# A transformer block on one core: FFN steps on 128 rows, a tabled order of the kernel's head, and other tables for PV

## The chip, the cores and the metric

The kernel runs on one core of a Trainium2 chip. The metric is the device time of one execution in microseconds (us), the median over several runs. TensorE (PE) does matrix products and loads its stationary operand in separate instructions (PEld); VectorE (DVE) and ScalarE (ACT) do elementwise work; GpSimd (POOL) does small operations and issues some DMAs; SyncE (SP) issues most DMAs and DMA transpositions.

## The reference

The block has 2048 rows of 1024 elements in bf16, an attention with 32 heads of 32 elements that share one K and one V, and a gated FFN with 3584 hidden elements.

```python
q = (ln(x) @ wq).reshape(B, S, 32, 32)           # 32 heads
k, v = ln(x) @ wk, ln(x) @ wv                    # one K and one V for all heads
p = softmax(einsum("bhqd,bkd->bhqk", q, k) * 32 ** -0.5)
h = x + einsum("bhqk,bkd->bhqd", p, v) @ wo
g, u = ln(h) @ w_gate, ln(h) @ w_up              # 1024 -> 3584 each
out = h + (sigmoid(g) * u) @ w_down
```

`ln` takes away a row's mean and divides by the root of its variance.

## The kernel before, in words

**Units.** Rows come in 16 tiles of 128 and 8 chunks of 256 (two tiles). Attention is cut into 64 groups; a group is one tile of 128 rows with 8 heads, in the order of the table ORDER, tile by tile after the first two. A group has 8 bursts, one for each 256 keys, so there are 512 bursts. `s_burst` (L658) is 8 score matmuls on 32 array rows each, four side by side; ACT then does two exps of 128x1024 (`one_exp`, L681). When a group's exps are there, `pv_group` multiplies them with V (L783, 32 array columns each, four side by side) and with ones for the softmax sum: either directly (L780) or, in groups that are `summed`, after DVE has added pairs of tiles (L722) and merged these sums (L731), in one or two sum items (L762). DVE then empties the bank (L801, L802), takes the reciprocal and multiplies into QT (L807 to L813).

**The other work.** K, V and Q projections (L323 on `zone`, where the transposed rows and wq lie), the output projection `wo_group` (L323 on `wo`), whose result is added to x (L873) and normalised (`stats2`, L904 to L913, POOL's powers at L349 and L351, L355), a DMA transposition of these rows on SP's queue (`transpose2`, L492), and the FFN of a chunk. A FFN step is one block of 256 hidden elements: gate (L971, then tanh on ACT, L990), up (L971, then the product on DVE, L1010). After 14 blocks come four down groups of 28 matmuls (L1035, added on DVE at L1045, stored from SP). Sigmoid is written through tanh.

**Memory.** PSUM has six banks for scores (S_ps) and two (X_ps) for everything else, so of PV, projections and FFN two groups are open at a time. The blocks of w_gate and w_up (512 KB each, "halves" in the code) are loaded on SP's queue into any free buffer of `halves`: four in wgu from the first chunk on, one more in QT after each chunk, nine in Pr and one in kT4 at the end. They are loaded anew for each chunk. w_down takes the place of the transposed rows and of wq in `zone`: 14 loads on POOL's queue (`load_wd`), each when its place is free.

**Order.** The program is written out by a planner at build time, which keeps a clock for each engine. The *head*, written out by hand, has the first 25 bursts: three groups side by side (HG = 3) and the first burst of the fourth. Each of its iterations p has three bursts, the V projection of 256 keys, two PV items of group 0, the K projection of the next keys and the normalisation of two more tiles (`ln1_step`). `zeros` are matmuls on a tile of zeros (L426). After the head a loop decides at each step what PE does next: a burst as soon as ACT is due for one; PV items; an open output group that is `first`; a new PV group; else the next group from `next_group`, which takes the output projection if its rows are ready, then what is left of q_list, then the FFN. The FFN's next step is taken when both tiles of its chunk are transposed and its block is expected within 0.3 us.

PV_PLAN has one letter for each attention group. c and e start a group right behind the first burst for which it is ready; d and e hold a burst back when the running PV group would be done within PV_HOLD; an upper case letter gives one sum item and one merge more instead of two sum items. `urgent(c)` tells that Q is done and the FFN has come to chunk c, with at most NEAR down groups to go; then output groups and their normalisation go first. WD_GAP is the number of bursts between w_down loads after Q is done. `dma` keeps a model of SP's transfers at 220 KB per us.

## Time and profile before

| | us |
|---|---|
| median of 3 runs | 1105.14 (1104.99 to 1105.42) |
| the profiled execution | 1105.36 |
| its span | 1103.5 |
| first exp starts / last exp ends | 13.8 / 1009.5 |
| last Q projection / first FFN matmul | 164.1 / 164.3 |
| first FFN matmul of chunks 1 to 7 | 294.4, 419.2, 543.5, 667.9, 791.9, 912.7, 1027.5 |
| transposition of the second tile of chunks 0 to 7 issued | 152.0, 280.3, 406.3, 530.0, 655.0, 779.4, 903.2, 1021.5 |
| last six w_down loads issued | 164.8, 175.6, 187.6, 200.1, 211.7, 223.6 |
| changes between score, PV and full matmuls on PE | 1101 |

The span is what the profile's parts cover; the execution's own time has 1.9 us around it. A busy share of PE holds the pipelined ends of matmuls, so how long one takes of PE is read from the distance of two starts, not from its duration. The granted clock is 1.00 in all stretches of the profile.

### The profile page before, as it was taken

Reading aid. Unit: us, or ns where it says so; the run is one execution under the profiler, and the core shown is the slowest. Engines: PE = TensorE matmul, PEld = TensorE weight load, DVE = VectorE, ACT = ScalarE, POOL = GpSimd, SP = SyncE. Lnnn points to the kernel's source line nnn. Section 1 sums busy time; section 2 is a strip of 40 time slices with the busy share of each in tenths; the row PEclk is TensorE's granted clock in tenths of the full one; section 3 lists DMA queues with packets and bytes.
Section 4 is the critical chain, followed back from the end, with each engine's and each line's share of the span. In section 5 each row is a group of like instructions: output and inputs, shape, how many; then the busy total and the mean of one; then the engine's idle time right before and its main releaser. Section 6 shows DMA issues by size and latency. Waiting matters only on the chain.

```text
span 1103.5 us, 32984 instructions
## 1 busy us (share of the span) xinstructions
PE 1077.9 (98%) x14253; PEld 659.5 (60%) x14315; DVE 876.1 (79%) x1574; ACT 1005.7 (91%) x1150; POOL 68.8 (6%) x142
## 2 busy tenths in 40 slices
PE   7899999999999999999999999999999999999998
PEld 6663446674476636674576546674576546674784
DVE  7769978888879888888888888888879888886111
ACT  6999999999999999999999999999999999995110
POOL 4510100100000000000000000000000000000000
PEclk9999999999999999999999999999999999999999
DMA  8951207681367515592276515582277515672920
GB/s 219 159 168 57 78 20 207 197 238 50 81 195 176 160 30 152 155 223 62 66 204 180 160 30 150 156 222 65 69 206 179 158 30 150 179 202 70 263 63 20
DMA packets 282065, 150.38 MB, mean 136 GB/s; under 512 B 38592, under 2 KB 276160, under 8 KB 281920
## 3 DMA queue, kind: packets, MB, share of 16 engines
q1 hardware_dynamic: 276256, 138.17, 47.3%
q0 software_dynamic: 2544, 9.44, 2.6%
q8 instruction: 113, 1.85, 0.7%
q10 hardware_dynamic: 3120, 0.66, 0.3%
q14 instruction: 32, 0.26, 0.1%
HBM read 136.18 MB, written 4.19 MB: 127 GB/s over the span
## 4 chain that ended last, share of the span: by engine, by line
PE 77%; ACT 10%; DVE 8%; issue 3%; POOL 1%; DMA 1%; DVEq 0%; ACTq 0%
PE X_ps L971 36%; PE X_ps L1035 13%; PE S_ps L658 12%; PE X_ps L783 8%; ACT Pr L681 8%; PE X_ps L323 7%; DVE pairs L731 3%; DVE pairs L722 2%; PE X_ps L762 1%; ACT hact L681 1%; DVE st L370 1%; ACT QT L681 0%; DMA zone<-hn 0%; PE X_ps L780 0%; DVE hx L873 0%
## 5 line engine op out<-in xcount | busy, mean ns | idle before, releaser
L681 ACT ACTIVATE Pr<-S_ps 128x1024 bf16<-128x1024 f32 x992 | 936.3, 1140 | 2.1 <-issue 1.3
L722 DVE TENSOR_TENSOR pairs<-Pr 128x1024 bf16<-128x1024 bf16 x479 | 324.3, 683 | 59.4 <-ACT Pr L681 56.4
L731 DVE TENSOR_TENSOR pairs<-pairs 128x1024 bf16<-128x1024 bf16 x397 | 273.6, 689 | 23.6 <-DVE pairs L722 0.5
L971 PE MATMUL X_ps<-QT,wgu 128*128 128x256 bf16 x2096 | 265.9, 273 | 0.1
L971 PEld LDWEIGHTS X_ps<-QT,wgu 128*128 128x128 bf16 x2096 | 193.1, 98 | 55.0 <-issue 31.3
L1035 PE MATMUL X_ps<-zone,hact 128*128 128x512 bf16 x850 | 207.0, 380 | 6.9 <-issue 5.6
L658 PE MATMUL S_ps<-QT,kT 32*128 32x256 bf16 x4096 | 203.4, 273 | 7.7 <-ACT kT L515 3.0
L971 PE MATMUL X_ps<-QT 128*128 128x256 bf16 x1328 | 167.4, 273 | 0.0
L658 PEld LDWEIGHTS S_ps<-QT,kT 32*128 32x128 bf16 x4096 | 60.9, 92 | 154.0 <-ACT Pr L681 133.4
L971 PEld LDWEIGHTS X_ps<-QT 128*128 128x128 bf16 x1328 | 123.7, 98 | 29.9 <-issue 15.6
L1035 PEld LDWEIGHTS X_ps<-zone,hact 128*128 128x128 bf16 x896 | 77.6, 97 | 102.4 <-issue 25.5
L783 PE MATMUL X_ps<-Pr,V 128*32 128x256 bf16 x3968 | 131.1, 273 | 0.9 <-DVE hact L1010 0.7
L990 ACT ACTIVATE gu<-X_ps 128x512 f32<-128x512 f32 x112 | 78.1, 698 | 57.6 <-PE X_ps L971 57.6
L1010 DVE SCALAR_TENSOR_TENSOR hact<-gu,X_ps 128x512 bf16<-128x512 f32 x112 | 76.3, 682 | 45.6 <-PE X_ps L971 44.7
L783 PEld LDWEIGHTS X_ps<-Pr,V 128*32 128x32 bf16 x3968 | 98.2, 96 | 21.7 <-issue 9.3
L323 PE MATMUL X_ps<-zone 128*128 128x512 bf16 (+3 forms) x576 | 77.9, 276 | 3.9 <-DMA zone<-hn 2.3
L323 PE MATMUL X_ps<-wo,QT 128*128 128x512 bf16 x240 | 61.4, 380 | 1.3 <-issue 0.8
L338 POOL CAST mean<-mv 128x1 f32<-128x1 bf16 x28 | 10.3, 366 | 825.1 <-DVE mv L908 815.1
L323 PEld LDWEIGHTS X_ps<-zone 128*128 128x128 bf16 x576 | 38.1, 97 | 33.9 <-issue 14.1
L801 DVE COPY ols<-X_ps 128x256 f32<-128x256 f32 x64 | 27.0, 421 | 26.3 <-PE X_ps L762 23.7
L1045 DVE SCALAR_TENSOR_TENSOR hx<-X_ps,hx 128x512 bf16<-128x512 f32 x32 | 21.9, 684 | 27.1 <-PE X_ps L1035 27.0
L323 PEld LDWEIGHTS X_ps<-wo,QT 128*128 128x128 bf16 x256 | 22.3, 97 | 28.6 <-issue 8.2
(76 smaller groups left out, 454.5 us busy)
## 6 DMA issues: line engine op xcount, KB each, us to landing
wgu<-in_B_w_gate_dram SPq DMA_DIRECT2D x73, 512.0 KB, 5.0
wgu<-in_B_w_up_dram SPq DMA_DIRECT2D x58, 512.0 KB, 4.9
QT<-in_B_w_up_dram SPq DMA_DIRECT2D x49, 512.0 KB, 5.0
QT<-in_B_w_gate_dram SPq DMA_DIRECT2D x34, 512.0 KB, 4.8
zone<-in_B_w_down_dram POOLq DMA_DIRECT2D x14, 512.0 KB, 5.4
hx<-in_A_x_dram SPq DMA_DIRECT2D x16, 256.0 KB, 4.3
out_dram<-hx SPq DMA_DIRECT2D x32, 128.0 KB, 1.7
Pr<-in_B_w_gate_dram SPq DMA_DIRECT2D x5, 512.0 KB, 7.1
```

What stands on the lines that cost most here:

```text
L323: ins = pe.matmul(sel(bank), lhsT=a, rhs=b, start=(i == 0), stop=(i == last))
L658: ins = pe.matmul(S_ps[:, bank, kt * QC:(kt + 1) * QC], lhsT=kT4[DH * j:DH * (j + 1), (2 * b + kt) * P:(2 * b + kt + 1) * P], rhs=QT[DH * ...
L681: c_e.inc(act.activation(out=p_tile(k, n % 2), in_=S_ps[:, 2 * pr:2 * pr + 2, :].rearrange("p a (b q) -> p (a b) q", q=QC), func=ACTF.Exp, ...
L722: add_half[k] = slot_use[slot] = c_dve.inc(dve.tensor_tensor(out=pairs[:, slot, :].rearrange("p (j q) -> p j q", j=4), in0=p4[:, :, 0, :], ...
L731: slot_use[x] = slot_use[y] = c_dve.inc(dve.tensor_tensor(out=pairs[:, x, :], in0=pairs[:, x, :], in1=pairs[:, y, :], op=ALU.add), T_ADD, ...
L783: ins = pe.matmul(bank[DH * j:DH * (j + 1), 0:QC], lhsT=V[:, 2 * b + kt, :], rhs=rhs(j), start=first and is_sum, stop=last and plain, tile ...
L801: dve.tensor_copy(out=ols[:, 0:QC], in_=bank[:, 0:QC])
L971: ins = pe.matmul(bank[:, j * QC:(j + 1) * QC], lhsT=halves[i][:, dt, j * P:(j + 1) * P], rhs=QT[:, dt, c * QC:(c + 1) * QC], start=(dt == ...
L990: tanh_val[n] = c_act.inc(act.activation(out=slot, in_=bank, func=ACTF.Tanh, scale=0.5), T_TANH, 0.1)
L1010: hact_val[(c, 2 * fp + 1)] = gu_read[n] = c_dve.inc(dve.scalar_tensor_tensor(out=hact[:, 2 * fp:2 * fp + 2, :], in0=slot.rearrange("p (a ...
L1035: ins = pe.matmul(bank, lhsT=hact[:, ft, tt * P:(tt + 1) * P], rhs=wd[:, ft, dc * 512:(dc + 1) * 512], start=(ft == 0), stop=(ft == NFT - 1))
L1045: v = c_dve.inc(dve.scalar_tensor_tensor(out=hv, in0=bank, scalar=0.5, in1=hv, op0=ALU.mult, op1=ALU.add), 0.61, 0.08)
```

## The change

**FFN steps.** The FFN's list now has pairs of blocks. When both tiles of a chunk are ready, a pair becomes gate, gate, up, up on 256 rows. When only the first tile is, it becomes one gate and one up group on 128 rows with both blocks in a bank, and a second such step for the other tile is put ahead of the chunk's down groups; its four blocks are loaded again, after the chunk's other loads. While that waits for the second tile, down groups of the first may run.

```diff
+                if x[0] == "pair":
+                    _, c, m = x
+                    ts, fs = UNITS[c], [2 * m, 2 * m + 1]
+                    if rows_ready(ts, now):
+                        if not halves_ready([(c, 0, 0, fs[0])], now):
+                            return None
                         ffn_list.popleft()
+                        n = [new_step(c, ts, [f], 0) for f in fs]
+                        ffn_list.extendleft([("u", n[1]), ("u", n[0]), ("g", n[1]), ("g", n[0])])
+                    elif rows_ready(ts[:1], now) and halves_ready([(c, 0, 0, f) for f in fs], now):
+                        ffn_list.popleft()
+                        n = new_step(c, ts[:1], fs, 0)
+                        ffn_list.extendleft([("u", n), ("g", n)])
+                        ffn_list.insert([i for i, y in enumerate(ffn_list) if y[0] == "down"][0], ("later", c, m))
+                        i = len([u for u in half_list if u[0] <= c])
+                        for u in reversed([(c, 1, w, f) for w in range(2) for f in fs]):
+                            half_list.insert(i, u)
...
-                            ins = pe.matmul(bank[:, j * QC:(j + 1) * QC], lhsT=halves[i][:, dt, j * P:(j + 1) * P],
-                                            rhs=QT[:, dt, c * QC:(c + 1) * QC], start=(dt == 0), stop=(dt == DT - 1))
+                            ins = pe.matmul(bank[:, j * m:(j + 1) * m], lhsT=halves[i][:, dt, j % 2 * P:(j % 2 + 1) * P],
+                                            rhs=QT[:, dt, r0:r0 + m], start=(dt == 0), stop=(dt == DT - 1))
```

`rows_ready` and `halves_ready` ask the planner's clock for the transposed rows and the blocks. Output groups are now listed by tile, and tile 1's are no longer always `first`.

**Head.** A table says what stands in each of its 21 places: V a V projection, u or U the next of HEAD_U and then of the eight 256-row groups of chunk 1's Q (u emptied by ACT, U by DVE), W the first 512-row Q group, P a PV item, L an `ln1_step`, z four zero matmuls.

```diff
+    HEAD = ['uuL', 'V', '', '', 'LVLu', 'UU', 'PP', 'LWL', 'zu', 'PPL', 'VV', 'uLPLz', 'PPVL', 'U', 'UPL', 'Pz', 'U', 'UP', 'PzP', 'VV', 'PPU']
+    HEAD_U = [5, 6, 4, 7]
...
             for p in range(1, BPG):
                 k0 = HG * p + 1
                 s_burst(k0)
                 exps(k0)
-                g1 = vq_group(p, [])
-                run_group(g1)
-                run_item(pv[0])
-                run_item(pv[0])
-                zeros(3, pv[0])
-                ln1_step(2 * p + 4)
+                head(3 * p - 2, p)
                 s_burst(k0 + 1)
                 exps(k0 + 1)
-                q = p + 2
-                if q > HG:
-                    g1 = vq_group(None, [q]) if q < NQ else q_group(q - NQ, QC, QC)
-                    run_group(g1)
-                zeros(5, pv[0])
-                ln1_step(2 * p + 5)
+                head(3 * p - 1, p)
                 s_burst(k0 + 2)
```

The third place of an iteration, behind the K projection, has `head(3 * p, p)` instead of five zero matmuls; place 0 stands ahead of the first K projection of the head.

**Tables and the planner's figures.**

```diff
-    PV_PLAN = "aedaEaaaadaaaaAABAaaEEEBCAEaEEEacbEaEEEaCAEEEEEacAdCAEEdaCEEEEEc"
+    PV_PLAN = "aaaaAcaaaACCaAEAaCCAEAAAaAEAaAAdaACAaAACaAAEaABCaAAEaABCaAAeAaac"
+    BANK_WAIT = 0.15
-    WD_AT, WD_GAP, WD_LATE = 6, 6, 6
+    WD_AT, WD_GAP, WD_LATE = 6, 2, 6
-                k_dma[0] = begin + kb / 220.0
+                k_dma[0] = begin + kb / 285.0
...
                 if pv_ready and (pe_mode[0] == "s" and plan not in "ce" or not can_s) and not (
-                        plan == "a" and busy(cur[0]) and cur[0].left() < 1.0):
+                        plan == "a" and busy(cur[0]) and cur[0].left() < 1.0) and not (
+                        busy(cur[0]) and cur[0].bank is not None and bank_time(1 - cur[0].bank) > k_pe[0] + BANK_WAIT):
```

In the planner's model a V matmul now counts 62 columns, where it counted 128.

More of the change, by code (lines that the diff above doesn't have):

```diff
@@ L1104, in _, with blocked @@
+            def blocked():
+                if q_list or not ffn_list or ffn_list[0][0] not in ("pair", "later"):
+                    return False
+                x = ffn_list[0]
+                return x[0] == "later" or not rows_ready(UNITS[x[1]][:1], k_pe[0])
             need(pe, warm_val)
@@ L1162, in ln1_step, with head @@
                     ln1_stats(t + 2)
-            ln1_step(4)
-            ln1_step(5)
+            def head(i, p):
+                for x in HEAD[i]:
+                    if x == "V":
+                        run_group(vq_group(v_next.pop(0), []))
+                    elif x == "X":
+                        kind, n = u_list.popleft()
+                        assert kind == "u"
+                        run_group(vq_group(v_next.pop(0), [n]))
+                    elif x == "W":
+                        run_group(q_group(*q_list.popleft()))
+                    elif x == "P":
+                        run_item(pv[0])
+                    elif x == "L":
+                        ln1_step(t_next.pop(0))
+                    elif x == "z":
+                        zeros(4, pv[0])
+                    else:
+                        unit(x == "u")
+            for c0 in range(512, S, 512):
+                q_list += [(q, c0, 512) for q in range(NQ)]
+            pv[0] = pv_group(0)
+            head(0, 0)
+            run_group(k_group(1))
+            exps(3, (1,))
+            for _ in range(2):
+                ln1_step(t_next.pop(0))
             for p in range(1, BPG):
```

214 lines of the change are left out of this document (126 added, 88 removed).

## The prediction

> **What bounds the kernel now.** I read the shares and the forty slices first, then the same busy times by stage, then the timelines of the head and of the tail.
>
> ```profile
> PE 1077.9 (98%) x14253; PEld 659.5 (60%) x14315; DVE 876.1 (79%) x1574; ACT 1005.7 (91%) x1150; POOL 68.8 (6%) x142
> ...
> PE   7899999999999999999999999999999999999998
> ...
> ACT  6999999999999999999999999999999999995110
> ```
>
> ```profile
> 13.40:62.00 48.60, 38.96 (x707) 27.47 (x711) 35.01 (x85) 45.71 (x55) 22.09 (x51) 1.00 0.89 183
> 62.00:164.00 102.00, 100.90 (x1473) 47.61 (x1471) 89.09 (x168) 101.94 (x112) 10.17 (x16) 1.00 0.21 69
> 164.00:1009.00 845.00, 835.02 (x11267) 510.31 (x11318) 723.46 (x1267) 843.18 (x964) 30.66 (x58) 1.00 0.53 143
> 1009.00:1103.00 94.00, 91.36 (x664) 63.00 (x662) 20.45 (x34) 8.91 (x15) 1.29 (x3) 1.00 0.42 108
> ```
>
> The columns are the stretch, its length, then busy time of PE, PEld, DVE, ACT and POOL, the clock and DMA. The first row is the head (25 score bursts with the projections of K and V), the second runs to the end of the Q projections, the third is FFN beside attention, the fourth the FFN alone. From 62 to 1009 PE and ACT are both full. ACT ends with its last exp at 1009.5 and PE works 94 us more. So the end is set by the sum of PE's work: an ACT that finishes later costs nothing as long as PE has FFN work to put beside it, and a microsecond taken off PE anywhere shortens the end, if PE never runs out of ready work. The chain of waits agrees (PE 77% of it, ACT 10%). Only in the head is PE idle, 9.6 of 48.6 us, and 4.2 us of what it counts as busy there is filler (below).
>
> ```profile
> 18.91 0.40 PE L658 MATMUL S_ps<-QT,kT 32*128 32x256 bf16 x8 [1.22 <-ACT wo L681]
> 20.61 1.03 PE L323 MATMUL X_ps<-zone 128*128 128x256 bf16 x8 [1.30 <-DMA zone<-hn]
> 21.48 0.44 PE L426 MATMUL X_ps<-pairs 128*128 128x128 bf16 x5
> 22.21 0.40 PE L658 MATMUL S_ps<-QT,kT 32*128 32x256 bf16 x8 [0.29 <-ACT kT L515]
> ```
>
> Start, length, line, and in brackets what PE waited for: a K projection waits for transposed rows, then five filler matmuls run (L426), then a burst waits for K.
>
> **The Q projections moved into the head.** Before, the head held four first-tile groups, the 256-row groups of q 0 and 1, and 75 of the 203 fillers. HEAD holds the same four, all eight 256-row groups and one 512-row group (W), and four `z` of four fillers. So six groups of eight 256-column and one of eight 512-column matmuls leave the stretch 62 to 164. In the timeline such matmuls follow each other at 0.110 and 0.217 us: 6 x 8 x 0.110 + 8 x 0.217 = 7.0 us of PE. They take the place of 59 fillers (75 less 16, at 0.056 us: 3.3 us) and of idle time; 3.3 + 9.6 = 12.9 us of room for 7.0. **-7.0.**
>
> Does the head grow? Its bursts go at ACT's pace: two exps start 0.904 us apart, 25 x 1.81 = 45.2 us, and K's evacuations. Five of the new groups (`u`) are evacuated by ACT, whose 0.38 us evacuation lets the next exp start 0.28 after it: 1.4 us. ACT idled 0.99, 0.54 and 0.70 us before three K evacuations; the first two `u` lie in the first of these gaps, the third ahead of the third. The other two add 0.28 each. Two groups between bursts (`UU`, 1.8 us against a free slot of 1.4) push a burst by 0.4, which the exp already queued hides. The row normalisations stay in the same order on DVE, with two or three evacuations of 0.4 between them. **+0.6**; ends -1 (the K waits shrink) and +3 (both X_ps banks: after the first PV item one bank serves K, V and Q one after the other, each behind a DVE evacuation).
>
> **The FFN order gate, gate, up, up** keeps instructions and evacuations (112 tanh, 112 products). A tanh gets one more group to finish in. 0, ends +-1.
>
> **PV tables.** Upper case letters save one sum item (four concurrent matmuls, 0.11 us): sum items go from 83 to 80, -0.3 us on PE; three more merges of 0.69 us on DVE (79%) are hidden. Letters d and e, which hold a burst back so that PV isn't cut, go from 29 to 7; a goes from 25 to 45. A change between burst, PV and full matmuls costs 0.096 us: 109 ns from one L971 matmul to the next, 205 from L971 to a burst. Following the 64 PV groups through the timeline, E groups come with 2.25 more changes than the work around them needs, a and A groups outside the head with about 3. Twenty groups x 0.75 x 0.096 = **+1.4**; with the sums +1.1. Ends -3 (1101 changes now, 1024 needed by 512 bursts; the search may find fits that I can't see) and +4 (two extra cuts per group).
>
> **BANK_WAIT.** A PV group no longer opens when the other bank is still being emptied. PE waited in nine of 77 entries from a burst into PV, 1.45 us together; **-1.0**, ends -2 and 0.
>
> **Half steps.** A step on 128 rows does two 256-wide F blocks with 32 matmuls of 128 columns; the second tile repeats it, and the four weight blocks are loaded again. In the head 28 matmuls of 128 columns took 1.74 us with a last one of 0.219: (1.74 - 0.22)/27 = 0.056 us. A pair of blocks in two halves is 128 x 0.056 = 7.2 against 64 x 0.110 = 7.0: +0.2 us.
>
> ```profile
> 13.70 1.74 PE L323 MATMUL X_ps<-zone 128*128 128x128 bf16 x28
> ```
>
> The Trainium skill speaks against this: TensorE: Matmul & The Clock Gate, section Back-to-back issue gap, gives about 81 ns sustained per pair of weight load and matmul at 128 columns. By that figure a pair would cost 128 x 81 ns, an estimate of 10.4 us. The trace disagrees, with 56 ns for such a stream.
>
> When do they run? Only when Q is done and the first tile's rows are transposed and the second's aren't. Tile 1's transposition is issued at 152.0, and takes some 3 us; the FFN starts at 164.3. Taking out 7 us of PE in a stretch where bursts and PV take a good third brings Q's end to about 154, so one or two pairs will be halved there. From chunk 1 to 5 the second tile lands 10 to 11 us ahead of the FFN (280.3 issued, 294.4 started), so these stay whole. In the tail they are what makes the 7 us count:
>
> ```profile
> 1017.62 10.09 PE L1035 MATMUL X_ps<-zone,hact 128*128 128x512 bf16 x45
> ...
> 1021.54 1.24 SPq L492 DMA_TRANSPOSE QT<-hn  x1
> ...
> 1027.55 1.91 PE L971 MATMUL X_ps<-QT,wgu 128*128 128x256 bf16 x16
> ```
>
> Chunk 6's down projection (L1035) covers tile 15's normalisation and its transposition, with about 3 us to spare. With 7 us less of it PE would stand idle from 1020 to 1024.5; two half pairs (7 us) of tile 14 fill that. Three to four pairs in all, +0.6 with both ends inside +-0.5, if weights are there.
>
> **Weights.** PE waits in order, so behind a late weight block stand the bursts, and behind these ACT. In 170 to 182 PE takes a block (512 KB) every 2.18 us; with a w_down load between them blocks land 1.8 us apart (180.17, 182.54, 184.06, 185.77, 187.36). Before, the last six w_down loads come every 11 us; WD_GAP 2 makes it 3.7. Then 22 us hold 6 + 10 loads of 1.8 = 28.8 us. The four buffers lead by about 2.6 us and PV groups give PE other work for some 3: 1 to 2 us short. POOL's waits there are for exps already queued. **+1.5** with the first half steps; ends 0 and +6.
>
> **Sum**, against the profiled execution's own 1105.36 us (span 1103.5, 1.9 around it): -7.0 + 0.6 + 1.1 - 1.0 + 0.6 + 1.5 = -4.2. The median of the runs is 0.2 lower: 1105.14 - 4.2 = 1100.9.
>
> **Rivals.**
> (a) *Weights late; slower.* With four buffers, a half pair uses its four blocks in 5 us, not 8.7, so PE comes to the next 3.7 us early; its four repeated loads take 7.2 us of DMA where PE wants them in 5. About 5.5 us for each pair halved in chunk 0, which has only the four. Two pairs are 11 us in place of my 1.5: 1110.4. One pair, 5.5 us, just takes the gain of 4.2 and the 1.5; from the second on it is slower. For it: the landings of 5.7 to 7.4 us in 174 to 181. Against: the kernel starts a step only when its model has the weights. 0.17.
> (b) *The tables give the gain back*: +4 for the changes in place of 1.4, and 1.6 more in the head: 1105.1, no change. For it: E's lower count in this trace. Against: the letters were counted in another order of work. 0.13.
> (c) *Half steps don't come about* (the second tile is in time, or the blocks aren't): the tail idles 4 of the 7 us, while 0.6 and some 1 us of weights fall away: 1103.3, same, near to faster. For it: the 3 us margin at 1025. 0.08.
> (d) *Narrow matmuls are bound by weight loads.* The profile's LDWEIGHTS rows last 98 ns; if they didn't overlap, a pair would cost 128 x (98 - 55) ns = 5.5 us, four pairs 22: 1122. The 56 ns in the head speaks against it. The skill's 81 ns lies on this side. 0.02.
> (e) *My forecast*: 0.60, own range 1096 to 1103.
>
> **Numbers.** Unknown ends reach from about -10 to +6 around the sum's middle; leaving out (d), the upper part of (a) and the lowest corner gives 1094.5 to 1106.5. Two tenths of a per cent, 2.2 us, is about what a measurement of this kernel can tell from none: faster is below 1102.9. Faster 0.60 + 0.02 from (c) + 0.03 from (b) = 0.65, same 0.16, slower 0.19.
>
> **What would show it.** Fillers 203 to 144; Q's last matmul at 152 to 157; the 25th burst within 1 us of 61.9; the last exp near 1010 with a tail near 87, not 94; L971 matmuls of 128 columns some 400 to 500, at 56 ns; mode changes about 1115; waits of L971 on DMA under 2 us. I am wrong if the last exp comes past 1013, if PE waits on weights after 155, or if the changes pass 1150.

## The result, and the profile after

The changed kernel takes 1113.15 us (median of four runs, 1111.43 to 1114.15) against 1105.14 before: a ratio of 1.0071 [1.0053, 1.0088], 8 us slower where 4.2 us faster was forecast. The profiled execution took 1112.62 us with a span of 1110.9 (before 1105.36 and 1103.5), so the span grew by 7.3 (1103.55 to 1110.88).

Shares and slices of the kernel after:

```profile
PE 1091.3 (98%) x15444; PEld 676.2 (61%) x15444; DVE 880.6 (79%) x1578; ACT 1010.5 (91%) x1155; POOL 67.0 (6%) x136
...
PE   7999999999999999999999999999999999999998
...
ACT  6999999999999999999999999999999999997110
...
q1 hardware_dynamic: 355296, 178.02, 63.8%
```

The shares look the same as before, and both PE and ACT did more. ACT falls off one slice later. Queue q1 moved 178.02 MB where it moved 138.17: 76 blocks of 0.524 MB were loaded twice, so 19 pairs were halved.

Busy time by stage, the columns as before (stretch, length, PE, PEld, DVE, ACT, POOL, clock, DMA share, GB/s), with the stretches cut at the after kernel's own 25th burst, last Q group, last exp and end:

```profile
13.40:65.50 52.10, 43.96 (x688) 28.22 (x692) 35.91 (x86) 47.92 (x60) 21.73 (x50) 0.93 0.81 171
65.50:147.00 81.50, 81.49 (x1188) 37.20 (x1188) 74.40 (x139) 81.22 (x90) 8.92 (x13) 1.00 0.25 83
147.00:165.00 18.00, 16.28 (x287) 10.27 (x286) 10.85 (x21) 16.20 (x19) 4.90 (x8) 1.00 0.79 209
165.00:1020.00 855.00, 852.35 (x12282) 526.32 (x12283) 731.44 (x1278) 849.89 (x969) 25.58 (x47) 1.00 0.69 177
1020.00:1110.60 90.60, 85.25 (x860) 62.73 (x852) 19.95 (x34) 9.45 (x16) 1.29 (x3) 1.00 0.73 181
```

The head is 3.6 us longer at a mean clock of 0.93. From 147 to 165, where the FFN now begins, PE and ACT both idle some 1.8 us. In the tail PE idles 5.3 of 90.6 us with the DMA at 0.73; 2.5 of these lie behind its last matmul, which ends at 1108.1.

Cut by events, the difference reads:

| from the traces, us | before | after | |
|---|---|---|---|
| 49th exp starts (end of the head) | 62.38 | 65.95 | +3.6 |
| from there to the end of the last exp | 947.2 | 955.1 | +8.0 |
| last exp ends | 1009.5 | 1021.1 | +11.5 |
| from there to the end of the span | 94.0 | 89.8 | -4.2 |
| exps 128 to 256 (FFN of chunk 0 begins here) | 124.4 | 128.7 | +4.3 |
| exps 256 to 384 (chunk 1) | 124.6 | 126.7 | +2.1 |
| exps 384 to 1023, by 128, mean | 124.7 | 125.0 | +0.3 |
| last Q matmul / first FFN matmul | 164.1 / 164.3 | 147.0 / 151.7 | |
| changes of PE's mode | 1101 | 1136 | |

So the last exp, which the forecast had near 1010, came 11.5 us late, and the tail gave back 4.2. From the 49th exp to the end of the last one, before and after:

```profile
62.38:1009.54 947.16, 935.93 (x12731) 557.87 (x12780) 813.07 (x1434) 945.27 (x1075) 40.83 (x74) 1.00 0.49 135
65.95:1021.08 955.13, 950.76 (x13784) 574.56 (x13776) 817.27 (x1439) 947.93 (x1075) 39.41 (x68) 1.00 0.66 169
```

ACT does the same 1075 instructions in both, the exps and 98 tanh. Before, it idled 1.9 us of this stretch; after, 7.2.

What PE did with the time follows from its matmuls' starts: counts times 0.216, 0.109 and 0.056 us for 512, 256 and 128 columns, 0.096 for a change of mode, and what is left of the time as waits, in which the slower matmuls at half clock are counted too (the trace of before lacks 62 matmul records; its matmuls are counted by their weight loads, of which none is missing).

| PE, after less before, us | Q | down | gate, up | zeros | changes | waits | other | sum |
|---|---|---|---|---|---|---|---|---|
| to the 25th burst | +7.0 | | | -4.2 | -0.2 | +0.9 | | +3.6 |
| to the last burst | -7.0 | +8.6 | +2.5 | | +3.5 | +0.6 | -0.3 | +7.9 |
| to the end | | -8.6 | +0.5 | | +0.1 | +3.9 | | -4.2 |

Seven us of Q left the middle, and 40 down matmuls (8.6 us) came in from the tail; beside that difference the middle grew by what halving and changes of mode cost.

### The profile page after: what moved, and what is told of

The parts are those of the page before. It is cut to its first block, busy times and chain, and to the rows that moved or that the text cites. A ratio compares the mean times of both kernels' runs of the same rounds, so it can differ in the third digit from the quotient of the medians.

```text
span 1110.9 us, 35395 instructions
## 1 busy us (share of the span) xinstructions
PE 1091.3 (98%) x15444; PEld 676.2 (61%) x15444; DVE 880.6 (79%) x1578; ACT 1010.5 (91%) x1155; POOL 67.0 (6%) x136
## 3 DMA queue, kind: packets, MB, share of 16 engines
q1 hardware_dynamic: 355296, 178.02, 63.8%
## 4 chain that ended last, share of the span: by engine, by line
PE 90%; DMA 4%; ACT 2%; DVE 2%; POOL 1%; issue 1%; DVEq 0%; SPq 0%; ACTq 0%
PE X_ps L994 35%; PE X_ps L1061 18%; PE S_ps L668 14%; PE X_ps L793 11%; PE X_ps L330 10%; ACT Pr L691 1%; PE X_ps L772 1%; DMA wgu<-in_B_w_up_dram 1%; PE X_ps L433 1%; DMA QT<-in_B_w_up_dram 1%; PE X_ps L790 1%; DMA Pr<-in_B_w_up_dram 1%; DMA QT<-hn 1%; DMA QT<-in_B_w_gate_dram 1%; ACT hact L691 1%; DMA zone<-in_A_wq_dram 1%
## 5 line engine op out<-in xcount | busy, mean ns | idle before, releaser
L732 DVE TENSOR_TENSOR pairs<-Pr 128x1024 bf16<-128x1024 bf16 x479 | 324.2, 684 | 62.4 <-ACT Pr L691 59.0
L994 PE MATMUL X_ps<-QT,wgu 128*128 128x256 bf16 (+1 forms) x2704 | 266.6, 248 | 4.5 <-DMA QT<-hn 2.0
L994 PEld LDWEIGHTS X_ps<-QT,wgu 128*128 128x128 bf16 x2704 | 204.7, 98 | 53.9 <-issue 32.4
L1061 PE MATMUL X_ps<-zone,hact 128*128 128x512 bf16 x896 | 217.9, 380 | 0.0
L994 PE MATMUL X_ps<-QT 128*128 128x128 bf16 (+1 forms) x1840 | 173.5, 243 | 1.9 <-DMA QT<-in_B_w_up_dram 1.3
L994 PEld LDWEIGHTS X_ps<-QT 128*128 128x128 bf16 x1840 | 133.0, 98 | 31.0 <-issue 20.3
L793 PE MATMUL X_ps<-Pr,V 128*32 128x256 bf16 x3968 | 135.9, 274 | 0.1
L1012 ACT ACTIVATE gu<-X_ps 128x512 f32<-128x512 f32 x112 | 74.2, 663 | 59.5 <-PE X_ps L994 58.9
L793 PEld LDWEIGHTS X_ps<-Pr,V 128*32 128x32 bf16 x3968 | 95.7, 96 | 25.7 <-issue 16.7
L811 DVE COPY ols<-X_ps 128x256 f32<-128x256 f32 x64 | 26.9, 421 | 24.6 <-PE X_ps L772 22.6
```

Of the source, the lines that this page charges most:

```text
L732: add_half[k] = slot_use[slot] = c_dve.inc(dve.tensor_tensor(out=pairs[:, slot, :].rearrange("p (j q) -> p j q", j=4), in0=p4[:, :, 0, :], ...
L793: ins = pe.matmul(bank[DH * j:DH * (j + 1), 0:QC], lhsT=V[:, 2 * b + kt, :], rhs=rhs(j), start=first and is_sum, stop=last and plain, tile ...
L811: dve.tensor_copy(out=ols[:, 0:QC], in_=bank[:, 0:QC])
L994: ins = pe.matmul(bank[:, j * m:(j + 1) * m], lhsT=halves[i][:, dt, j % 2 * P:(j % 2 + 1) * P], rhs=QT[:, dt, r0:r0 + m], start=(dt == 0), ...
L1012: tanh_val[n] = c_act.inc(act.activation(out=slot, in_=bank, func=ACTF.Tanh, scale=0.5), T_TANH, 0.1)
L1061: ins = pe.matmul(bank, lhsT=hact[:, ft, tt * P:(tt + 1) * P], rhs=wd[:, ft, dc * 512:(dc + 1) * 512], start=(ft == 0), stop=(ft == NFT - 1))
```

## The experiments

Each was timed in three rounds beside the kernel before on its chip; ratios are to that kernel.

### What bounds the stretches

The forecast rested on PE's sum: a later ACT costs nothing, and a microsecond off PE anywhere counts. The rival is that bursts stand at fixed places in PE's queue and wait for exps, so that a delay of ACT passes to the end.

**act_late**: the kernel before, with three copies of 128x1024 (read by nobody) put on ACT at the end of the head.

```diff
+            need(act, *[xn_val[t] for t in (12, 13, 14, 15)], x_val[15])
+            for t in (12, 13, 14):
+                c_act.inc(act.activation(out=x_tile(t), in_=x_tile(15), func=ACTF.Copy))
```

> The kernel before with three more ACT copies of 128x1024 (dead data, of no use to the result) between the head and the loop, at about 62 us; the order of all other work is untouched. Three occupy ACT for 3 x 0.9 = 2.7 us. The premise of my prediction, that the sum of PE's work sets the end and a later ACT costs nothing: 1105 to 1105.6, with the tail behind the last exp 2.7 us shorter. Rival, which I now hold: bursts stand at fixed places in PE's queue and wait for exps, so in a stretch where both engines are full a delay of ACT delays all of PE's work behind the next burst: the last exp 2.5 us later, the tail as long as before, 1107.5 to 1108.

1108.67 us, 1.0026 [1.0015, 1.0037]; the profiled span grew by 3.9. ACT's timeline there, and the stretch of lower clock:

```profile
62.45 2.21 ACT L681 ACTIVATE QT<-S_ps 128x1024 bf16<-128x1024 f32 x2
64.26 3.20 ACT L1197 ACTIVATE gu<-gu 128x1024 bf16<-128x1024 bf16 x3
67.10 4.03 ACT L681 ACTIVATE Pr<-S_ps 128x1024 bf16<-128x1024 f32 x4
72.12 6.52 ACT L681 ACTIVATE Pr<-S_ps 128x1024 bf16<-128x1024 f32 x7 [0.99 <-PE S_ps L658]
```

```profile
68.40:71.80 3.40, 3.36 (x51) 1.64 (x51) 1.56 (x4) 2.73 (x3) 0.00 (x0) 0.51 0.00 0
```

The copies hold ACT 2.84 us (64.26 to 67.10). PE meanwhile waits 2.5 us for an exp, its clock is granted at 0.50 for the 3.4 us from 68.4, and ACT then waits 0.99 for PE: 3.8 together. The 49th exp starts at 62.45 as before, the last one ends 3.9 later, and the tail is unchanged at 94.0. Nothing was absorbed in 947 us. The three executions with a granted clock of 1.0 over the whole span took 1107.8 to 1108.8, 2.4 to 3.4 us more than the kernel before; the four at 0.997 took 1108.2 to 1110.5. The first half of the premise falls: an ACT that finishes later costs about all of it.

**b_light_q**: the kernel before, which leaves out half of the products of eight Q groups in the stretch 62 to 164 (its result is therefore not the block's, as in the next two).

```diff
-            def mm_list(pairs, sel, n):
+            def mm_list(pairs, sel, n, skip=()):
...
+                        if i in skip:
+                            k_pe[0] += n * T_MM
+                            return None
...
+                               (1, 3, 5, 6) if c0 == 1536 else ())
```

> The kernel before, with the same order of work; only the eight 512-row Q groups of rows 1536 to 2047 do four of their eight matmuls (half of that contraction is left out). It takes 32 x 0.217 = 6.9 us of PE out of the stretch 62 to 164, as the change did, but moves and adds nothing. The prediction's premise (a microsecond taken off PE anywhere shortens the end): 1105.1 - 6.9 = 1098.2, last exp 1002 to 1003, tail 94. The rival (ACT is full from 62 to 1009, and bursts wait for it at fixed places in PE's queue): PE waits for exps instead, last exp 1008 to 1010, 1104 to 1105.5.

1105.43 us against 1105.39, 1.0000 [0.9990, 1.0009]. Windows, and PE's waits from 62 to 170:

```profile
62.00:164.00 102.00, 95.19 (x1444) 44.88 (x1447) 88.91 (x167) 101.94 (x112) 10.17 (x16) 1.00 0.22 69
164.00:1009.00 845.00, 834.53 (x11265) 510.15 (x11316) 723.48 (x1268) 843.19 (x964) 30.66 (x58) 1.00 0.53 143
```

```profile
PE S_ps L662 <- ACT Pr L685: 6.1, 11, 0.9
```

PE's 100.90 became 95.19, ACT's 101.94 stayed, and PE waits 6.1 us for exps, where it waited 0.2 in this stretch before. The rival holds in full: in 62 to 164 a microsecond off PE is worth nothing. The order of work was frozen here; the change could still gain if other work of PE came forward into the place, which the later runs look at.

**b_light_act** and **b_light_both**: the kernel before with half of most tanh, alone and with the cut of Q above.

```diff
-act.activation(out=slot, in_=bank, func=ACTF.Tanh, scale=0.5)
+act.activation(out=slot if n < NGU else slot[:, 0:256], in_=bank if n < NGU else bank[:, 0:256], func=ACTF.Tanh, scale=0.5)
```

> The kernel before, same order of work; the tanh of all but the first four FFN blocks works on 256 of its 512 columns (half of the gate's activation is left out). Before, a tanh of 512 columns holds ACT 0.477 us and an evacuation of 256 columns 0.28, so some 0.2 us go from each of the 94 tanh that lie ahead of the last exp: 19 us of ACT. The prediction's premise (PE's sum sets the end): 1105. If ACT alone set it: 1086. Theory now (both are full, and PE idles only some 11 us of 62 to 1009): PE takes over after a few us, last exp 1000 to 1006, 1096 to 1102.

> Both cuts: half of the tanh and half of the eight Q groups of rows 1536 to 2047 (6.9 us of PE, worth 0.0 us alone). If PE has become the bound once ACT is lightened, the same 6.9 us now count: 4 to 7 us below the kernel with the light tanh alone, 1090 to 1097. If ACT still bounds the stretch 62 to 164, where only 14 or fewer tanh lie, they are worth nothing there again: within 1 us of the kernel with the light tanh.

The light tanh gave 1103.76, 0.9987 [0.9978, 0.9997]: 1.5 us, less than my theory's range. Both cuts gave 1104.39, 0.9994 [0.9985, 1.0003]: the cut of Q was worth nothing again. Windows of the kernel with the light tanh:

```profile
62.00:164.00 102.00, 101.00 (x1472) 47.66 (x1469) 89.31 (x168) 101.93 (x112) 10.16 (x16) 1.00 0.22 69
164.00:1009.00 845.00, 842.85 (x11343) 511.09 (x11342) 722.30 (x1268) 833.30 (x964) 30.66 (x58) 1.00 0.52 144
```

From 164 to 1009 ACT now idles 11.7 us and PE 2.2: PE took over after 1.5 us. The forecast's row has 10 us of idle PE in that stretch. Most of it was not there; PE's waits from 62 to 1009 in the trace of before, and its down projections (L1035) from 164 to 1009:

```profile
PE X_ps L1035 <- issue: 5.4, 34, 0.2
PE X_ps L323 <- issue: 0.8, 5, 0.2
```

```profile
164.00:1009.00 845.00, 168.38 (x677) 60.32 (x718) 1.00 0.53 143
```

718 weight loads have 677 matmuls on record, so the 39 gaps of 0.2 us (6.2 us) are matmuls whose records are missing; the kernel with the light tanh has no such gaps. This gives the picture that the other runs fit: **ACT alone bounds 62 to 164; from 164 to 1009 ACT is full too (1.8 us idle), and PE is so near to it that it takes over after 1.5 us.** Work can be added to neither. In no traced kernel with the whole of ACT's work did the stretch from the 49th to the last exp take less than the 947 us of before; with the light tanh it took 945.8. That PE is full there is read from the windows: no run took work off PE in this stretch.

### The head

The head grew by 3.6 us. Theories: the clock, which was granted at 0.50 for 6.8 us from 26.5 once the fillers were gone; the one X_ps bank that is left after the first PV item; ACT's five evacuations. The head's timeline after, in the place shown of before:

```profile
26.27 0.41 PE L668 MATMUL S_ps<-QT,kT 32*128 32x256 bf16 x8 [1.44 <-ACT Pr L691]
27.04 1.87 PE L330 MATMUL X_ps<-zone 128*128 128x256 bf16 x8 [0.36 <-DMA zone<-zone]
29.47 0.62 PE L668 MATMUL S_ps<-QT,kT 32*128 32x256 bf16 x8 [0.56 <-ACT kT L522]
```

The K projection takes 1.87 where it took 1.03, and the next burst 0.62 instead of 0.40.

**b_nofill**: the kernel before without its 91 zero matmuls of the head.

```diff
-            zeros(5, pv[0])
+            zeros(0, pv[0])
...
-                zeros(3, pv[0])
+                zeros(0, pv[0])
```

> The kernel before without the 91 zero matmuls in the head (PV's bank is opened as before); nothing else differs. Theory: these keep the granted clock up; without them it falls to 0.50 for one or two stretches of 3.4 us between 20 and 40 us, K projections and bursts there take twice as long, the 25th burst comes 1 to 2.5 us later than 61.9, and the time is 1106 to 1107.7. Rival: the clock falls but ACT paces the head and hides it, or it doesn't fall at all: 1105.

1106.51 us, 1.0008 [0.9999, 1.0017]. The clock:

```profile
20.80:34.50 13.70, 11.46 (x144) 6.12 (x141) 12.21 (x29) 11.06 (x13) 9.85 (x23) 0.50 1.05 238
```

It was 0.50 for 13.7 us; the 25th burst came at 62.95 instead of 61.90, and the end 1.0 later. So without the fillers the clock stays down for longer, and in the profiled execution the head's 1.0 went through to the end whole; over all executions the interval just takes in 1. The fillers don't hold the clock at all times: with the very head of before, it was 0.50 for 3.4 us from 20.7 in act_late and for 6.8 us from 19.6 in b_newpv. These falls moved the 49th exp by 0.1 us (62.45 and 62.48 against 62.38).

**fill**, **early_q**: the kernel after with three `z` back and one normalisation moved in the head's first iteration, or with two of the new Q groups moved there.

```diff
-    HEAD = ['uuL', 'V', '', '', ...
+    HEAD = ['uuL', 'VzL', 'z', 'z', ...
```

```diff
-    HEAD = ['uuL', 'V', '', '', ..., 'UP', 'PzP', 'VV', 'PPU']
+    HEAD = ['uuL', 'VU', 'U', '', ..., 'P', 'PzP', 'VV', 'PP']
```

> The changed kernel with three groups of four zero matmuls in the head's first iteration (PV's bank open from there on) and the normalisation of tile 6 behind that iteration's V projection, as before the change. Theory: the granted clock stays at 1.0 in the head, the 25th burst is at 63.3 to 64.3 instead of 65.5, and the time 1111 to 1112, as far as the gain is passed on; the rest of the head's growth (five evacuations on ACT, 1.4 us, and the single bank) stays. Rival, that the single bank from the first iteration on costs what the clock gives: the 25th burst at 65 to 66, 1113.

> The changed kernel with two of the head's Q groups (q 0 and 1, rows 256 to 511) moved from late in the head to its first iteration, where the changed kernel has no filler and one V group only; nothing else differs. Theory: the granted clock fell to 0.50 from 26.5 to 33.4 us because taking out the zero matmuls left PE too empty from 20 to 27 us (3.83 us of 7 busy, 4.21 before); with 1.7 us more work there the clock stays at 1.0, the 25th burst starts 1.5 to 2 us earlier (63.5 to 64 instead of 65.5) and the time is 1110 to 1112. Rival, that the head grew by the bank and by ACT's evacuations alone: the clock may stay up, but the 25th burst stays within 0.5 us of 65.5 and the time at 1113.

1114.86 us, 1.0080 [1.0063, 1.0096], and 1113.43, 1.0077 [1.0060, 1.0094]. Both missed: the clock fell all the same (6.8 us from 26.9; 3.4 us from 27.7), and the 49th exp came at 67.6 and 67.1. That `z` and Q groups hold the banks there is my reading; no run shows it by itself.

**fill2**, **fill2_dve**: fillers that give their bank back at once (six groups of eight, 48 matmuls; the expectation says seven and 56), and the same with the five evacuations on DVE.

```diff
-    HEAD = ['uuL', 'V', '', '', 'LVLu', ...
+    HEAD = ['uuL', 'Vff', 'ff', 'f', 'LVLuf', ...
...
+                    if x == "f":
+                        fill(8)
```

> The kernel after with seven groups of eight zero matmuls (128 columns, 56 in all) back in the first iteration of the head; they take a free bank, leave it without an evacuation, and the planner does not see them, so that the order of everything else stays that of the kernel after. Theory that two of the head's 3.6 us are the clock that fell to 0.50 when the fillers went: clock 1.0 through the head, 25th burst at 63.2 to 63.8 instead of 65.5, time 1110.8 to 1111.8. Rival that the banks and evacuations alone hold the head back: clock 1.0 or not, 25th burst 65 to 66.5, time 1112.5 to 1114.5.

> The same, and the five groups that ACT evacuated in the head are evacuated by DVE. If these evacuations cost ACT 0.28 us each in the head, the 25th burst comes 1.4 us earlier than with the fillers alone. The rival is that DVE, which also normalises the rows there, then holds the banks longer: no earlier, or up to 1 us later. The rest of the kernel is planned anew from the head's new times with a table that was not made for it, so only the head is compared; the time may be 2 to 8 us longer.

1116.65 us, 1.0096 [1.0079, 1.0113], and 1120.55, 1.0133 [1.0118, 1.0149]; only their heads are compared. With fill2 the clock stayed at 1.0 through the head, and the 25th burst came at 65.50, as late as without. The chain of work there:

```profile
26.47 0.38 PE S_ps L668 x8
26.85 2.31 issue
29.16 1.03 PE X_ps L330 x8
```

The K projection ran in 1.03 again but began 2.1 us later: the transposition of its rows, issued at 23.93, landed at 29.07 (5.1 us; 3.15 us in the kernel after, 26.90). What the clock gave back, a late transposition took, so the run does not settle what the clock costs in this head. It does show that a clock of 1.0 is not enough to bring the head back. More can be read from five kernels whose heads are the same instruction for instruction: the 49th exp came at 64.72 with 3.4 us at half clock (no_half), at 65.95, 65.82 and 66.52 with 6.8 us (after, gap6, no_half_last) and at 66.54 with 10.2 us (refit_no_half). So 6.8 us at half clock instead of 3.4 go with 1.1 to 1.8 us, 10.2 us with no more than that, and 2.3 of the 3.6 us are there with 3.4 us alone. The four executions of the result go the same way: 1111.43 at a mean clock of 0.998, 1112.62 at 0.997, 1113.69 and 1114.15 at 0.995. fill2_dve refutes the theory of ACT's evacuations as something that could be had more cheaply: with them on DVE the 49th exp came at 68.3, 2.3 us later still.

What the rest of the head's growth is made of stays open. From exp to exp the 3.6 us come in some six pieces of 0.3 to 1.3 us.

### The half steps

**no_half**, **no_half_last**: the kernel after with no half steps, or with none in the last chunk.

```diff
-                    elif rows_ready(ts[:1], now) and halves_ready([(c, 0, 0, f) for f in fs], now):
+                    elif False and rows_ready(ts[:1], now) and halves_ready([(c, 0, 0, f) for f in fs], now):
```

(`c < NU - 1` in place of `False` for the second.)

> The changed kernel with the branch that starts a chunk's FFN on its first 128 rows taken out; a pair of blocks waits for both tiles. Theory A: 19 half pairs cost more than they give: 1216 matmuls more that cost 2.9 us of PE, 76 weight blocks loaded again with some 5 us of PE waits at 150 to 175 and 1070 to 1090, and about 0.5 us a chunk of extra mode changes; without them PE idles at most 3 us at the start of a chunk, and only where bursts and PV don't fill it: 1106 to 1110. Rival B: the FFN now reaches each chunk ahead of its second tile, and what half steps fill (about 4 us a pair, 19 pairs) comes back as idle PE and as a later end: 1118 to 1125.

> The changed kernel with half steps in all chunks but the last; the order of work is the same up to the last chunk. Theory: the last chunk's FFN can't begin at 1030.7 but waits for tile 15's transposition, issued at 1033.5 and landed at 1039.9, so PE idles some 6 us there; its eight to twelve repeated blocks are gone and with them the 5.3 us of waits for weights at 1070 to 1090 and 0.6 us of narrow matmuls: 1112 to 1115. Rival one, half steps in the tail bring 5 us net: 1118. Rival two, they cost: 1109.

1117.55, 1.0114 [1.0099, 1.0129], and 1116.84, 1.0102 [1.0087, 1.0118]: with this table and head, half steps bring 3.7 to 4.4 us. The three pairs of the last chunk alone bring 3.7 of it, so nothing clear of noise is left for the other 16. Without the last chunk's the tail is 93.1 us instead of 89.8, and PE waits from 1022 on:

```profile
PE X_ps L994 <- issue: 5.3, 1, 5.3
```

That is the gap that the forecast saw (1020 to 1024.5). In the kernel after, half steps fill it:

```profile
1028.96 1.89 PE L1061 MATMUL X_ps<-zone,hact 128*128 128x512 bf16 x8
1030.68 1.95 PE L994 MATMUL X_ps<-QT 128*128 128x128 bf16 x32
1032.47 1.06 PE L994 MATMUL X_ps<-QT,wgu 128*128 128x128 bf16 x16
```

and their reloaded blocks are late afterwards; PE's waits from 1020 on there:

```profile
PE X_ps L994 <- DMA QT<-in_B_w_up_dram: 1.3, 2, 0.8
PE X_ps L994 <- DMA wgu<-in_B_w_gate_dram: 0.8, 1, 0.8
PE X_ps L994 <- DMA Pr<-in_B_w_up_dram: 0.7, 2, 0.5
```

**gap6**: the kernel after with w_down loads as far apart as before.

```diff
-    WD_AT, WD_GAP, WD_LATE = 6, 2, 6
+    WD_AT, WD_GAP, WD_LATE = 6, 6, 6
```

> The changed kernel with 6 bursts instead of 2 between the last six w_down loads. Theory: these loads beside the first FFN steps made the second tile's transposition take 7.6 us and weight blocks 6.3 to 9.3, so PE waited some 4 us in 150 to 175; with a gap of 6 the transposition takes under 5 us, PE's waits there fall to 1 to 2 us and the time is 1110 to 1111. Rival, that the repeated blocks of the half steps alone crowd the queue: waits stay at 3 to 4 us and the time at 1113. A second rival, that down groups come before w_down is loaded: a new wait near 233 us and 1115.

1112.08 us, 1.0061 [1.0046, 1.0076], about 1 us less, which lies within the two intervals and misses the 1110 to 1111 expected. Exps 128 to 256 took 127.2 us instead of 128.7. The theory's other half fell: the transposition of chunk 0's second tile, expected under 5 us, still took 7.4.

That chunk's loss in the kernel after, in its timeline:

```profile
155.63 3.26 SPq L499 DMA_TRANSPOSE QT<-hn  x1
...
158.98 1.34 PE L994 MATMUL X_ps<-QT,wgu 128*128 128x128 bf16 x17
159.15 0.72 POOL L238 DMA_DIRECT2D zone<-in_B_w_down_dram  x1 [3.40 <-ACT Pr L691]
...
163.23 0.83 PE L994 MATMUL X_ps<-QT,wgu 128*128 128x256 bf16 x6 [1.64 <-DMA QT<-hn]
...
164.42 1.94 ACT L691 ACTIVATE Pr<-S_ps 128x1024 bf16<-128x1024 f32 x2 [1.80 <-PE S_ps L668]
```

The FFN began 12.6 us earlier than before and met rows that weren't there. Tile 1's transposition was issued at 155.63 and landed at 163.18, 7.6 us later (3.0 before), between weight blocks that took 6.3 to 9.3 us. PE waits 1.64 for it, behind PE the next burst, and behind the burst ACT 1.80. With w_down spread out but the half steps kept it took 7.4 (gap6), with w_down close but no half steps 6.0 (no_half), and with neither 3.0 (refit_no_half, another table): w_down alone doesn't make it slow.

### Tables and fits

**old_head**, **b_newpv**: the kernel after with the old head, and the kernel before with the new PV table.

```diff
-    HEAD = ['uuL', 'V', '', '', 'LVLu', 'UU', 'PP', ...
-    HEAD_U = [5, 6, 4, 7]
+    HEAD = ['z', 'VPPzL', 'zL', 'z', 'VPPzL', 'UzL', 'z', ...
+    HEAD_U = [4, 5, 6, 7]
```

```diff
-    PV_PLAN = "aedaEaaaadaaaaAABAaaEEEBCAEaEEEacbEaEEEaCAEEEEEacAdCAEEdaCEEEEEc"
+    PV_PLAN = "aaaaAcaaaACCaAEAaCCAEAAAaAEAaAAdaACAaAACaAAEaABCaAAEaABCaAAeAaac"
```

> The changed kernel with the head's table filled in as the head was before (V, two PV items, fillers and two normalisations an iteration, the four first-tile groups and two Q groups; ACT evacuates none of them; four fillers at a place instead of three or five). Theory: the head takes 61.9 us again and the 7.0 us of Q come back behind it, so PE has 3.4 us more to do in all, but the FFN begins some 12 us later and most half pairs, with their 0.15 us each and their reloads, fall away: 1110 to 1114. Rival, that the head is the whole loss: 1105. Second rival, that the PV table fits only the new head: 1118 or more.

> The kernel before with the PV table of the changed kernel alone (the three merges more and sum items fewer with it). Theory: a letter belongs to one place in the order of work; set into another order the table gives 20 to 40 mode changes more (0.096 us each) and cuts groups where output groups and FFN wait for them: 1109 to 1117. Rival, that the letters as such cost 0.07 us a group as I counted: 1106 to 1107.

1127.0, 1.0191 [1.0176, 1.0207], and 1118.92, 1.0117 [1.0102, 1.0132]. A table in an order of work that it wasn't made for costs some 13 us (b_newpv against the kernel before) or 14 (old_head against the kernel after, although the head itself is 3.8 us shorter there). So the change's parts can't be priced by swapping one: each swap also breaks the table.

**refit_old_head**, **refit_no_half**, **refit_neither**, **refit2**: so the table was searched anew for three reduced changes: half steps allowed but the old head; the new head without half steps; neither. All have WD_GAP 6 and one DMA queue for all loads in the planner's model. refit2 is the first with another table.

```diff
-    WD_AT, WD_GAP, WD_LATE = 6, 2, 6
+    WD_AT, WD_GAP, WD_LATE = 6, 6, 6
...
-                    c.at[c.n] = CLK[id(q)][0] + 2.0 + kb / 100.0
+                    k_dma[0] = max(CLK[id(q)][0], k_dma[0]) + kb / 285.0
+                    c.at[c.n] = k_dma[0] + 2.0
```

(Beside the HEAD of old_head or the `False` of no_half, and PV_PLAN: "AAdadAEa..." for the first, "aAabeeBA..." for the second, "EABbceda..." for the third, "bBdEAacA..." for refit2.)

> The changed kernel with half steps and with the head as it was before, a gap of 6 for w_down, POOL's loads counted in the planner's model of transfers, and a PV table searched anew for this kernel by changing letters at random and keeping what ends sooner by the planner's clock. Theory: with a table of its own the old head is no loss: the 25th burst at 62, the last exp at 1009 to 1014, fewer than 19 half pairs, 1102 to 1109, that is 18 or more faster than the same head with the foreign table (1127.0). Rival, that the old head itself costs: 1113 or more.

> The changed kernel with its new head and without half steps, with the same gap and model and a PV table searched anew for it. Theory: the head's 2.4 us (as in the run without half steps, 64.7 against 62.4 for the 49th exp) go straight to the end and the FFN waits for tile 1 at 155 to 163; else as before: 1107 to 1111. Rival, that half steps are needed with this head whatever the table: 1115 to 1119.

> The changed kernel with the old head and without half steps, the same gap and model and a PV table searched anew; what is left of the change is the order gate, gate, up, up, the bank rule and the planner's figures. Theory: as the kernel before within the scatter of tables: 1102 to 1108. Rival, that gate, gate, up, up costs in itself: 1110 or more, with waits of up groups for banks in the FFN.

> The code after (half steps allowed) with the old head, WD_GAP 6 and a PV table searched longer for that order than that of the first such kernel (1106.5). If the table is what matters once the head is the old one: 1103 to 1105, as early as the kernel before or a little earlier, last exp 1008 to 1009.5, tail 93 to 94, no half steps. If the kernel before already has what ACT allows (idle 21 of 1010 us), any further table gives 1105 to 1107.

| | us | ratio | 49th exp | last exp ends | tail | halved pairs |
|---|---|---|---|---|---|---|
| before | 1105.14 | | 62.4 | 1009.5 | 94.0 | 0 |
| refit_old_head | 1106.52 | 1.0011 [1.0001, 1.0020] | 62.2 | 1010.8 | 93.4 | 0 |
| refit2 | 1107.01 | 1.0014 [1.0005, 1.0023] | 62.2 | 1014.6 | 89.6 | 1 |
| refit_neither | 1108.52 | 1.0033 [1.0022, 1.0044] | 62.0 | 1014.0 | 93.8 | 0 |
| refit_no_half | 1110.38 | 1.0045 [1.0030, 1.0060] | 66.5 | 1016.3 | 92.5 | 0 |
| after | 1113.15 | 1.0071 [1.0053, 1.0088] | 66.0 | 1021.1 | 89.8 | 19 |

refit_old_head and refit_neither differ by the table alone, since no pair was halved in either: tables found by search scatter by 2 us. Against refit_old_head the new head of refit_no_half costs 3.9 us, and its head is 4.4 longer: what the head lost went to the end, and Q's absence from the middle gave nothing that stands out of the tables' scatter. No fit came below the kernel before, and refit2, whose table was searched longer, not below the first.

refit_no_half also bears on chunk 0's loss. Its Q ended as early as in the kernel after (147.7), and its FFN waited for the rows until 160.3:

```profile
147.50:160.30 12.80, 10.53 (x205) 5.47 (x202) 6.31 (x12) 12.80 (x15) 2.76 (x5) 1.00 0.28 63
```

PE idles 2.3 us in this wait, and ACT not at all; exps 128 to 256 took 125.1 us, 0.7 more than before. refit_neither, with the old head, took 129.0. So Q's early end doesn't cost chunk 0 its 4.3 us by itself.

## Why the prediction was wrong

**The step that failed** is the premise that the sum hangs on: "an ACT that finishes later costs nothing as long as PE has FFN work to put beside it, and a microsecond taken off PE anywhere shortens the end". Both halves are refuted where the change acts: 3.8 us of delay on ACT at 64 cost 3.9 at the end, and 6.9 us off PE in 62 to 164 were worth 0.0. The forecast calls PE and ACT "both full" from 62 to 1009 and then goes by PE alone (100.90 of 102), though ACT has the shorter idle time in the same row (101.94 of 102). That a queue in fixed order hands each wait on to the engine that it feeds was in the text (under Weights), but not in the premise.

By PE's account the miss of 11.5 us in the profiled span (7.3 longer instead of 4.2 shorter) is 3.0 of the head, 2.4 of half steps, 2.1 of tables and changes, and 4.0 of waits behind the head, for rows and weights above all. The two accounts fit together: the stretch from the 49th to the last exp can't be shorter than ACT's work, so what Q leaves there only makes room for other work of PE, and each stall that reaches ACT lengthens it. Term by term:

- **Q into the head, -7.0, and its growth, +0.6.** Q's last matmul came 17 us earlier, 147.0, below the 152 to 157 foreseen, so the move was made. The head has 75 zero matmuls less (128 left; the head had 91 before, not the 75 that the forecast counted, hence its 144), which frees 4.2 us, but PE's waits in it didn't shrink: 15.3 us after 14.4, with what half clock adds. That the 7 us would fit into idle time was wrong, since that time lies ahead of K projections and bursts that wait for rows, banks and ACT. The head grew by 3.6, just beyond the upper end of +3, and since ACT bounds what follows, all of it stays.
- **What filled Q's place.** With the Q groups gone, down projections came forward, 8.6 us of them out of the tail. That is the only place where the change gains: the tail is 4.2 us shorter, where the forecast had 7 (94 to 87). Chunks 0 and 1 lost 6.4 us. The timeline of chunk 0 shows an FFN that starts early, meets unready rows and slow transfers, and holds up bursts behind its waits. The early end of Q isn't enough for that, as refit_no_half shows (0.7 us lost in chunk 0); what half steps, w_down loads and the table each add stays open.
- **Half steps, +0.6 with three to four pairs.** The price was right: 128-column matmuls follow each other at 0.056 us in L994 as in the head, and a pair costs 3.0/19 = 0.16 us more (0.2 foreseen). Rival (d) and the 81 ns of the Trainium skill (TensorE: Matmul & The Clock Gate, Back-to-back issue gap) are refuted by the 0.056. The number of pairs was wrong: 19, 2432 matmuls, since from chunk 1 on, too, the FFN was ahead of the rows (chunk 1 started at 281.5, its second tile's transposition was issued at 285.9). The forecast had said that these stay whole.
- **Weights, +1.5.** About right in chunk 0 (PE waited 1.0 us in 150 to 182 for blocks, and gap6 gave about 1 back), but the tail's 3.7 us of waits (by the distance of starts) for reloaded blocks were not foreseen. Rival (a) priced them at 5.5 us for each halved pair of chunk 0; one pair was halved there, and chunk 0 lost 4.3. Its mechanism was there, and its place was the tail too.
- **PV tables, +1.1.** Changes of mode went from 1101 to 1136, +3.4 us, inside the bounds and near rival (b); there are three sum items fewer, as said (316 matmuls of L772 after 328 of L762). I priced the letters one by one, and b_newpv shows that they have no price by themselves.
- **BANK_WAIT, -1.0.** By the distance of starts, PE's waits from a burst into a PV group between the 25th and the last burst went from 1.9 us to 0.0. But PE's waits there rose by 0.6 in all, and six other kernels with the same rule still have 0.3 to 3.0 us of such waits, so the rule alone doesn't take them away.

Of the signs named, the last exp past 1013 came true (1021.1), PE's waits on weights after 155 as well; the changes stayed under 1150. 1113.15 lies beyond every rival but (d), whose mechanism didn't occur: all were priced as sums of PE's work, with no case in which the head and the middle grow and nothing absorbs it. Rival (a) comes nearest (1110.4), in part by luck: it put the whole loss into chunk 0's waits, with two pairs halved there.

What stays open: how the part of the head's 3.6 us that doesn't go with the clock divides between rows and banks, what chunk 0's loss is made of, and what a table found for after's order by a longer search would give, since tables alone scatter by 2 us.

## What to carry to other kernels

In a stage table, look for the engine with the least idle time in each row before pricing anything: a cut on another engine is worth nothing there until work from a later, unbound stage is pulled into the gap, and what is pulled must have its inputs ready. When two engines are full and one feeds the other in a fixed order, a delay passes nearly whole to the end (3.9 us in act_late, 1.0 in b_nofill), so an edit has to be priced by the sum of delays along the order, not by one engine's sum. A table that was searched for one order is part of that order; a part of such a change can't be judged by swapping it alone.

## What the hardware showed beside that

**The clock fell although PE was a tenth to over half busy.** Every fall that ended within a kernel's span lasted 3.4 us or a multiple of it (6.8, 10.2, 13.7) at 0.50. In the 3.4 us ahead of it PE had been busy 1.12 us (after, 23.1 to 26.5), 0.87 (b_nofill, from 17.4), 0.98 (act_late, 65.0), 0.91 (fill2, 160.5), 0.71 (no_half_last, 1031.5), and in the extremes 0.31 (fill2_dve, 164.6) and 1.92 (refit_no_half, 21.4). No threshold comes out of this: in the kernel before, 0.89 us from 17.2 on were not followed by a fall. The Trainium skill (TensorE: Matmul & The Clock Gate, Part 1: The HAM clock gate) gives two states, 4/8 and 8/8, in windows of about 3.4 us, and the lengths and the 0.50 agree; it calls the window that throttles idle, and here none was idle. So a wait can be paid twice: in act_late 2.5 us of PE's waiting were followed by 3.4 us at half clock, in which ACT lost another 1.0.

**A transposition by DMA took 3.0 us alone and 7.6 among weight loads** (155.63 after; 151.96 before), and the same one of the head took 3.15 us in the kernel after and 5.1 in fill2. The forecast had given it some 3.

**Missing records look like idle time.** 41 matmuls of L1035 had no record in the trace of before, and the 0.2 us gaps that they left (6.2 us with those of L323) looked like room on PE. The count of weight loads beside that of matmuls shows it.
